# Rows of expert tiles turned by VectorE in 32x32 blocks instead of by TensorE, loaded in five pieces instead of one

## The chip, the cores and the metric

The kernel runs on one core of a Trainium2 chip. The metric is the device time of one execution in microseconds; the profile is of one execution, and its span is the time between its first and last instruction. TensorE (PE), VectorE (DVE), ScalarE (ACT), GpSimd (POOL) and SyncE (SP) each work through a queue of their own in order. SP computes nothing here: it reads registers from tables and issues most of the DMAs.

## The reference

A long convolution, done by Fourier transforms, is followed by a mixture of experts in which each token goes to the one expert with the highest score.

```python
batch, seq, d_model = (8, 5696, 128)          # x; h is (seq, d_model)
N, D, E, F = (45568, 128, 8, 1024)            # w_gate (D, E), w1 (E, D, F), w2 (E, F, D)
...
Xf = np.fft.rfft(x, n=L, axis=1)
Hf = np.fft.rfft(h, n=L, axis=0)
y = np.fft.irfft(Xf * Hf[None, :, :], n=L, axis=1)[:, :S, :]
...
logits = x @ w_gate
expert_idx = np.argmax(logits, axis=1)
...
h = np.maximum(xe @ w1[e], 0.0)
ye = h @ w2[e]
out[mask] = gate_w[mask, None] * ye
```

## The kernel before, in words

The batch is cut in three groups of 2, 3 and 3 sequences. Each goes through a forward transform (`phase_a`), a product with the filter's spectrum (`phase_b`) and the way back with the scoring of tokens (`phase_c`). At the end of `phase_c` GpSimd scatters each token as a row of 130 words into `SR` in DRAM, sorted by expert: 128 values, the gate and the token's index. So each group gives a part of the sorted rows.

`experts()` works on tiles of T = 256 rows, all of one expert, 37 tiles in the first part; 182 tiles lie in the main loop. It runs beside the phases of the later groups: a small scheduler written in Python (`run`) interleaves the generators by costs, and fixes the order of each engine's queue at build time. Once the last group's rows are sorted, expert tiles run alone to the end.

A tile j goes as follows. `load` reads its row number from a table that the chip has computed (`tab`), into a register of SP, and issues the load of 256 rows into a buffer `xr`, two rows to a partition, some three tiles ahead (`ahead(j + 3)`). There are XR = 19 such buffers, used in turn; a few tiles use other free room (`spares`). `turn` makes TensorE flip the two 128x128 halves against an identity matrix (`flip`) into a PSUM bank `mx`, whose other half takes the flips of a finished output `ot`; `turned_in` splits the result into a rounded part (ScalarE) and a rest (VectorE), together `xtb`. Four steps k = 0 to 3 follow: `layer1` fills a PSUM bank `mh` (two of these), `relu` reads it on ScalarE and then on VectorE into `hs`, and two steps later `layer2` adds into `ma`. `drain` copies the sums to `ot`, `turn` flips them back, and `emit` multiplies them by the gate and writes them over the rows in `xr`. `place` later scatters them to `out` by the index that came with the row, two scatters of 128 rows a tile.

Rows of tile j + 1 are turned in step k = 2 of tile j, in the same `turn` as the output of tile j - 1:

```python
jo = j3 if k3 == NPAIR - 1 else None
ji = j + 1 if k == LAG and j + 1 in rows else None
```

The weights of a tile's expert come in four loads `wb` from `WD` (`load_w`), each on the condition that the expert has changed. Up to tile TWO = 76 a tile's weights are asked for one tile ahead, from there two tiles ahead into a second set of buffers. For them SP reads two more numbers of the table. A load waits for the readers of its buffer, and SP's whole queue with it. The DMAs that SP issues signal in turn on eight semaphores, so that each also waits for the one eight before it.

Of the kernel before, what the change touches and what calls it, by code (L numbers as in the profile page):

```python
# [28 lines left out]
T = 256  # L29
# [29 lines left out]
RARE = 3  # L59
TWO = 76  # L60
STEP = 1065
XR = 19
PACE = (1800, 2200)
ROOM = 28
REST = (224, 288, 288)
QUICK = (1, 1, 1)
TABLED = 4
RATE = (0.372, 0.55, 0.28, 0.8, 1.05, 0.6)


@with_exitstack
def conv_moe(ctx: ExitStack, tc: tile.TileContext, I, out, B, S, D, E, F, split):
    nc = tc.nc
# [627 lines left out]

    outs, pending, held = [], [], []

    def place(xr, s, after=None):
        sc = nc.gpsimd.indirect_dma_start(  # L705
            out=out[:, :],
            out_offset=IndirectOffsetOnAxis(ap=xr[:, s, D + 1 : D + 2].bitcast(I32), axis=0),
            in_=xr[:, s, :D],
            in_offset=None,
            bounds_check=B * S - 1,  # L710
            oob_is_err=False,
        ).ins
        tc.declare_no_dep(sc, group="out", reason="each token is written once")
        tc.add_to_no_dep_group("out", sc)
        if len(outs) >= PIPE_LANES:
            tc.add_manual_dep(sc, outs[-PIPE_LANES].name, SYNC, reason="scatter lane")
        if after is not None:
            tc.add_manual_dep(sc, after.name, SYNC, reason="results leave one by one")
        outs.append(sc)

    def spread(done, behind=0):
        gap, now = PACE[0 if state["tail"] else 1], state["pe"] + behind
        if now - state["sent"] < gap:
            return
        if len(pending) > (ROOM if state["space"] else 0):
            place(*pending.pop(0), done.ins)
        elif held and not state["space"]:
            place(*held.pop(0), done.ins)
        else:
            return  # L730
        state["sent"] = now
# [247 lines left out]
    def tables(pt):  # L979
# [62 lines left out]
        tab = const.tile([1, 3, NT], I32, name=f"tab{g}")  # L1042
# [28 lines left out]
        pt.tab = tab  # L1071
# [42 lines left out]
    def experts():  # L1114
# [2 lines left out]
        later, cycle = set(), []  # L1117
        seq = [(pt, j) for pt in parts for j in range(pt.nt)]

        def load(i):  # L1120
            pt, j = seq[i]
            r0 = nc.sync.value_load(pt.tab[0:1, 0, j : j + 1], min_val=0, max_val=E * CAP)
            xr = next(state["spare"], None) if state["spare"] else None
            if xr is None:
                while len(cycle) >= XR and any(o[0] is cycle[-XR] for o in pending):
                    place(*pending.pop(0))
                xr = sb.tile([P, 2, RW], F32, tag="xr", name=f"xr{i}", bufs=XR)
                cycle.append(xr)
            else:
                later.add(i)  # L1130
            ld = nc.sync.dma_start(xr, SR[ds(r0, T), :].rearrange("(p s) w -> p s w", s=2)).ins
            tc.declare_no_dep(ld, group="sr", reason="reads rows that are complete", keep=pt.ends)
            tc.add_to_no_dep_group("rows", ld)
            for s in pt.ends:
                tc.add_manual_dep(ld, s.name, SYNC, reason="all rows are sorted")
            rows[i] = xr

        def turns(i):
# [6 lines left out]
            return wbuf[turns(i), n]  # L1145

        def load_w(i, n):
            pt, j = seq[i]
            if n == 0:
                ew = nc.sync.value_load(pt.tab[0:1, 1, j : j + 1], min_val=0, max_val=(E - 1) * P)  # L1150
                ch = None
                if i and i != TWO + 1:
                    ch = nc.sync.value_load(pt.tab[0:1, 2, j : j + 1], min_val=0, max_val=1)
                regs[i] = (ew, ch)
            ew, ch = regs[i]
# [8 lines left out]
            if n == 3:  # L1164
                regs.pop(i)

        xbank, hbank, obank = {}, {}, {}

        def turn(jo, ji):
            bank = ps.tile([P, 2, 2, P], F32, tag="mx", name=f"mx{jo}_{ji}", bufs=1)  # L1170
            if jo is not None:
                ot = ots.pop(jo)
                for s in range(2):
                    flip(bank[:, 0, s], ot[:, s * P : (s + 1) * P], P)
                obank[jo] = bank[:, 0]
            if ji is not None:
                for s in range(2):
# [48 lines left out]

        def emit(j):
            op, xr = obank.pop(j), rows.pop(j)
            nc.vector.tensor_tensor(
                out=xr[:, :, :D], in0=op, in1=xr[:, :, D : D + 1].broadcast_to([P, 2, D]), op=ALU.mult  # L1230
            )
            if j in later:
                held.extend((xr, s) for s in range(2))
            else:
                pending.extend((xr, s) for s in range(2))

        def tiles(lo, hi):
            LAG = 2
            steps = [(j, k) for j in range(lo, hi) for k in range(NPAIR)]
            hss, wants, due = {}, [], [lo]  # L1240

            def pump():
                while wants and seq[wants[0][0]][0].ready:
                    load_w(*wants.pop(0))

            def want(i, n):
                if i < hi:
                    wants.append((i, n))
                    pt, j = seq[i]
                    if i == TWO or (i == lo and i > TWO and i + 1 < hi):  # L1250
                        wants.append((i + 1, n))
                    pump()

            def ahead(i):
                while due[0] <= min(i, hi - 1) and seq[due[0]][0].ready:
                    load(due[0])
                    due[0] += 1

            while not seq[lo][0].ready:
                yield None  # L1260
            for n in range(4):
                want(lo, n)
            ahead(lo + 2)
            if lo == 0:
                yield LULL
            M = len(steps)
            for n in range(M + LAG + 1):
                j, k = steps[n] if n < M else (None, None)
                j2, k2 = steps[n - LAG] if 0 <= n - LAG < M else (None, None)
                j3, k3 = steps[n - LAG - 1] if n >= LAG + 1 else (None, None)  # L1270
                if k is not None:
                    while not seq[j][0].ready:
                        yield None
                    pump()
                    ahead(j + 3)
                    if j not in xts:
                        turn(None, j)
# [201 lines left out]
```

## Time and profile before

| | us |
|---|---|
| median of 3 runs | 2128.43 |
| lowest and highest | 2121.01, 2129.2 |
| profiled execution | 2119.45 |
| its span | 2117.4 |
| TensorE busy | 2046.9 (97%) |
| VectorE busy | 1563.5 (74%) |
| GpSimd busy | 1347.3 (64%) |
| ScalarE busy | 1119.5 (53%) |

Busy times of TensorE are those of its matmul rows, which overlap; the time that one holds the engine is read from the starts of rows that follow each other. SP's register work and issues are not in the table, since the profile doesn't count them as busy.

### The profile page before, as it was taken

Reading aid. Unit: us, or ns where it says so; the run is one execution under the profiler, and the core shown is the slowest. Engines: PE = TensorE matmul, PEld = TensorE weight load, DVE = VectorE, ACT = ScalarE, POOL = GpSimd, SP = SyncE. Lnnn points to the kernel's source line nnn. Section 1 sums busy time; section 2 is a strip of 40 time slices with the busy share of each in tenths; the row PEclk is TensorE's granted clock in tenths of the full one; section 3 lists DMA queues with packets and bytes.
Section 4 is the critical chain, followed back from the end, with each engine's and each line's share of the span. In section 5 each row is a group of like instructions: output and inputs, shape, how many; then the busy total and the mean of one; then the engine's idle time right before and its main releaser. Section 6 shows DMA issues by size and latency. Waiting matters only on the chain.

```text
span 2117.4 us, 47410 instructions
## 1 busy us (share of the span) xinstructions
PE 2046.9 (97%) x14548; PEld 1779.0 (84%) x14548; DVE 1563.5 (74%) x3520; ACT 1119.5 (53%) x2333; POOL 1347.3 (64%) x1575
## 2 busy tenths in 40 slices
PE   9999999799999999979999999999999999999998
PEld 6799777477777777767888888888889999999998
DVE  5699677799997788889888887677785555555554
ACT  5677555255554544435666665444444444454544
POOL 6576288755554388888998886288884444444333
PEclk9999999799999999999999999999999999999999
DMA  8899799999996898867768775757634144443331
GB/s 268 260 294 304 227 310 284 245 238 228 244 240 194 229 292 254 255 180 209 181 182 221 208 188 149 196 142 205 176 103 143 54 134 136 132 133 130 122 124 34
DMA packets 215138, 415.63 MB, mean 196 GB/s; under 512 B 31797, under 2 KB 135531, under 8 KB 214884
## 3 DMA queue, kind: packets, MB, share of 16 engines
q1 hardware_dynamic: 186703, 357.00, 59.3%
q0 software_dynamic: 27072, 55.35, 9.0%
q8 instruction: 118, 1.93, 0.4%
q14 instruction: 136, 1.11, 0.2%
q10 hardware_dynamic: 1109, 0.23, 0.1%
HBM read 571.44 MB, written 154.27 MB: 343 GB/s over the span
## 4 chain that ended last, share of the span: by engine, by line
PE 78%; DVE 9%; DMA 6%; POOL 3%; issue 2%; ACT 2%; SPq 0%; POOLq 0%; DVEq 0%; ACTq 0%
PE mh L166 22%; PE ma L166 21%; PE vp L166 8%; PE xp L166 8%; PE yp L166 5%; PE pa L166 4%; PE mx L191 3%; POOL SR L687 2%; DMA SR<-rt,pi 1%; DMA uq<-U 1%; DVE hs L1202 1%; DMA wb<-WD 1%; PE lb L191 1%; PE tp L191 1%; PE gb L166 1%
## 5 line engine op out<-in xcount | busy, mean ns | idle before, releaser
L1202 DVE SCALAR_TENSOR_TENSOR hs<-mh,hs 128x512 fp32r<-128x512 f32 x728 | 500.4, 689 | 352.2 <-ACT hs L1200 345.7
L166 PE MATMUL mh<-xtb,wb 128*128 128x256 f32 x4368 | 703.2, 296 | 16.4 <-DVE hs L1202 9.0
L1200 ACT ACTIVATE hs<-mh 128x512 fp32r<-128x512 f32 x728 | 435.6, 599 | 466.7 <-PE mh L166 463.1
L166 PEld LDWEIGHTS mh<-xtb,wb 128*128 128x128 f32 x4368 | 585.9, 189 | 86.2 <-issue 29.9
L166 PE MATMUL ma<-hs,wb 128*128 128x256 f32 x4368 | 653.1, 285 | 3.5 <-DMA wb<-WD 3.5
L166 PEld LDWEIGHTS ma<-hs,wb 128*128 128x128 f32 x4368 | 569.3, 189 | 4.8 <-DMA wb<-WD 4.5
L705 POOL DMA_INDIRECT out<-xr x310 | 305.4, 985 | 347.7 <-ACT hs L1200 164.0
L687 POOL DMA_INDIRECT SR<-rt,pi x384 | 397.8, 1036 | 186.7 <-ACT hs L1200 80.6
L586 POOL TENSOR_TENSOR zt<-zt,xs 128x384 f32<-128x384 f32 (+1 forms) x282 | 300.9, 1069 | 132.2 <-DVE xs L575 93.4
L579 DVE TENSOR_TENSOR xs<-xp,hh 64x384 f32<-64x384 f32 (+1 forms) x360 | 214.7, 596 | 7.8
L623 ACT COPY vt<-vp 96x384 f32<-96x384 f32 x240 | 114.0, 475 | 180.9 <-PE vp L166 177.1
L166 PE MATMUL vp<-zt,mi 128*96 128x384 f32 x480 | 196.2, 490 | 0.7 <-PE xp L166 0.7
L570 DVE TENSOR_TENSOR zt<-xp,hh 128x384 f32<-128x384 f32 (+1 forms) x300 | 173.2, 577 | 25.0 <-PE xp L166 14.7
L166 PE MATMUL xp<-uq,mt 96*128 96x384 f32 (+1 forms) x496 | 173.5, 453 | 16.5 <-DMA uq<-U 10.3
L166 PE MATMUL pa<-xc,fcr 120*120 120x512 f32 x576 | 159.1, 410 | 2.2 <-POOL xc L298 1.0
L166 PE MATMUL yp<-vq,gcs 120*120 120x384 f32 x384 | 140.3, 487 | 4.1 <-ACT ut L331 2.7
L575 DVE SCALAR_TENSOR_TENSOR xs<-xp,hh 64x384 f32<-64x384 f32 x240 | 134.2, 559 | 4.2
L920 POOL MEMSET spent<- 120x288 f32 (+1 forms) x366 | 127.4, 348 | 0.5
L166 PEld LDWEIGHTS pa<-xc,fcr 120*120 120x120 f32 x576 | 98.8, 185 | 25.8 <-DVE rk L909 3.9
L166 PEld LDWEIGHTS xp<-uq,mt 96*128 96x128 f32 x496 | 86.1, 196 | 38.9 <-issue 21.6
L166 PEld LDWEIGHTS vp<-zt,mi 128*96 128x96 f32 x480 | 78.5, 164 | 48.0 <-issue 25.2
L331 DVE COPY ut<-pa 120x512 f32<-120x512 f32 x96 | 65.6, 683 | 64.1 <-PE pa L166 52.8
(168 smaller groups left out, 2587.7 us busy)
## 6 DMA issues: line engine op xcount, KB each, us to landing
wb<-WD SPq DMA_DIRECT2D x728, 512.0 KB
U<-ut SPq DMA_DIRECT2D x48, 720.0 KB
uq<-U SPq DMA_DIRECT2D x60, 576.0 KB
V<-vt SPq DMA_DIRECT2D x60, 576.0 KB
vq<-V SPq DMA_DIRECT2D x48, 720.0 KB
xt<-x SPq DMA_DIRECT2D x96, 240.0 KB
xr<-SR SPq DMA_DIRECT2D x155, 130.0 KB
WD<-wsp SPq DMA_DIRECT2D x32, 512.0 KB
```

The source lines that it names most:

```text
L166: nc.tensor.matmul(to, lhs, rhs, **kw)
L191: nc.tensor.transpose(dst, src, ident[:n, :n])
L570: nc.vector.tensor_tensor(out=zt, in0=x3, in1=hv[:, 0].broadcast_to([P, PK, cb, D]), op=ALU.mult)
L575: nc.vector.scalar_tensor_tensor(out=xs[to, 0], in0=x3[at, 0], scalar=-1.0, in1=him[:, 0], op0=ALU.mult, op1=ALU.mult)
L579: nc.vector.tensor_tensor(out=xs[to], in0=x3[at], in1=him, op=ALU.mult)
L586: eng.tensor_tensor(out=zt, in0=zt, in1=xs, op=ALU.add)
L623: done = nc.scalar.copy(outs_[qb][:, k0 : k0 + PK, c * cw : (c + 1) * cw], banks.pop(n)[:K2, :iw].rearrange("p (q x) -> p q x", q=PK),)
L687: s = nc.gpsimd.indirect_dma_start(out=SR[:, :], out_offset=IndirectOffsetOnAxis(ap=pi[:, b : b + 1], axis=0), in_=rt[:, b, :], in_offset= ...
L705: sc = nc.gpsimd.indirect_dma_start(out=out[:, :], out_offset=IndirectOffsetOnAxis(ap=xr[:, s, D + 1 : D + 2].bitcast(I32), axis=0), in_=x ...
L920: nc.gpsimd.memset(spent[:, : REST[g]], 0.0)
L1200: done = nc.scalar.activation(hs[:, 0], hp, AF.Relu)
L1202: done = nc.vector.scalar_tensor_tensor(out=hs[:, 1], in0=hp, scalar=0.0, in1=hs[:, 0].bitcast(F32), op0=ALU.max, op1=ALU.subtract)
```

## The change

From tile QUAD = 37 on, which is the first tile of the second part, the rows are loaded in five DMAs. Four bring 32 channels each, with the 256 rows as eight blocks of 32 to partitions of their own; the fifth brings gate and index, 8 bytes a row. One VectorE instruction then turns all 32x32 blocks, and since the blocks already lie where the full transpose needs them, the result `xf` is the turned tile. It lies in SBUF, not in PSUM, and no input flip is left on TensorE. The turning moves from step 2 to step 1 of the tile before, and stands on VectorE ahead of that step's `relu`. A partition's two rows are now 128 apart instead of neighbours, so `emit` and `place` see the buffer through `views`. For all tiles, the table is laid out with the three numbers of a tile side by side and read into SP's registers by one instruction (`numbers`). One row buffer gives its room to `xf`.

```diff
-XR = 19
+XR = 18
...
+QUAD = 37
...
+    def views(xr, quad):
+        if not quad:
+            return xr[:, :, :D], xr[:, :, D : D + 1], xr[:, :, D + 1 :]
+        flat = xr.rearrange("p s w -> p (s w)")
+        rest = flat[:, 2 * D :].rearrange("p (s w) -> p s w", w=2)
+        return flat[:, : 2 * D].rearrange("p (s d) -> p s d", d=D), rest[:, :, :1], rest[:, :, 1:]
...
+        def numbers(i):
+            if i not in regs:
+                pt, j = seq[i]
...
+                got = nc.values_load_multi_w_load_instructions(
+                    pt.tab[0:1, j], [mybir.EngineType.SP], min_val=0, max_val=E * CAP, skip_runtime_bounds_check_because=why
+                )[1]
...
         def load(i):
             pt, j = seq[i]
-            r0 = nc.sync.value_load(pt.tab[0:1, 0, j : j + 1], min_val=0, max_val=E * CAP)
+            r0 = numbers(i)[0]
...
+            if i >= QUAD:
+                flat = xr.rearrange("p s w -> p (s w)")
+                for k in range(4):
+                    src = SR[ds(r0, T), k * 32 : (k + 1) * 32].rearrange("(b p) f -> p b f", p=32)
+                    dst = flat[k * 32 : (k + 1) * 32, : 2 * D].rearrange("p (b f) -> p b f", f=32)
+                    moves.append(nc.sync.dma_start(dst, src).ins)
+                src = SR[ds(r0, T), D:].rearrange("(s p) w -> p s w", p=P)
+                moves.append(nc.sync.dma_start(flat[:, 2 * D :].rearrange("p (s w) -> p s w", w=2), src).ins)
...
-            if n == 0:
-                ew = nc.sync.value_load(pt.tab[0:1, 1, j : j + 1], min_val=0, max_val=(E - 1) * P)
...
-                    ch = nc.sync.value_load(pt.tab[0:1, 2, j : j + 1], min_val=0, max_val=1)
...
+        def blocks(j):
+            xbank[j] = sb.tile([P, T], F32, tag="xf", name=f"xf{j}", bufs=1)
+            nc.vector.transpose(xbank[j], rows[j].rearrange("p s w -> p (s w)")[:, : 2 * D])
...
-                ji = j + 1 if k == LAG and j + 1 in rows else None
+                ji = j + 1 if k is not None and k == (1 if j + 1 >= QUAD else LAG) and j + 1 in rows else None
...
-                if jo is not None or ji is not None:
-                    turn(jo, ji)
+                early = ji is not None and ji >= QUAD
+                if jo is not None or ji is not None and not early:
+                    turn(jo, None if early else ji)
...
                 yield 1420
+                if early:
+                    blocks(ji)
                 if k is not None:
                     hss[n] = relu(j, k)
```

VectorE's queue late in the program, where expert tiles run alone, one tile before the change (`hs_0` to `hs_3` are the four steps' buffers, `mx` the PSUM bank of the flips):

```order
L1202 SCALAR_TENSOR_TENSOR hs_1_26283<-mh_1_26270,hs_1_26283 128x512
L1202 SCALAR_TENSOR_TENSOR hs_2_26330<-mh_2_26311,hs_2_26330 128x512
L1185 TENSOR_TENSOR xtb_26336<-mx_109_26318,xtb_26336 128x256
L1229 TENSOR_TENSOR xr_25780<-mx_109_26318,xr_25780 128x2x128
L1202 SCALAR_TENSOR_TENSOR hs_3_26353<-mh_3_26340,hs_3_26353 128x512
L1202 SCALAR_TENSOR_TENSOR hs_0_26385<-mh_0_26372,hs_0_26385 128x512
```

The same place after the change, in VectorE's queue (line numbers have shifted by 30):

```order
L1232 SCALAR_TENSOR_TENSOR hs_0_25383<-mh_0_25370,hs_0_25383 128x512
L1209 STREAM_TRANSPOSE xf_25399<-xr_25160 128x256
L1232 SCALAR_TENSOR_TENSOR hs_1_25401<-mh_1_25386,hs_1_25401 128x512
L1215 TENSOR_TENSOR xtb_25407<-xf_25399,xtb_25407 128x256
L1232 SCALAR_TENSOR_TENSOR hs_2_25431<-mh_2_25414,hs_2_25431 128x512
L1260 TENSOR_TENSOR xr_24959<-mx_None,xr_24959 128x256
L1232 SCALAR_TENSOR_TENSOR hs_3_25451<-mh_3_25438,hs_3_25451 128x512
```

The transpose stands between the `hs` of steps 0 and 1, and the subtraction that makes `xtb` has moved from behind step 2's `hs` to behind step 1's.

SP's queue in the same place before the change, from one tile's first table read to its weight loads (an ISA row is work on registers; semaphore instructions and moves are not listed):

```order
L1122 TENSOR_LOAD tab_25033
L1122 ISA x2
L1131 ISA
L1131 DMA xr_28966<-SR 128x260
L1150 TENSOR_LOAD tab_25033
L1150 ISA x2
L1153 TENSOR_LOAD tab_25033
L1153 ISA x2
L1163 ISA
L1163 DMA wb_0_20374<-WD 128x1024
```

And after the change, SP's queue from the one table read to the first weight load's register work:

```order
L1133 TENSOR_LOAD tab_23308
L1159 ISA
L1159 DMA xr_27887<-SR 32x8x32
L1159 ISA
L1159 DMA xr_27887<-SR 32x8x32
L1159 ISA
L1159 DMA xr_27887<-SR 32x8x32
L1159 ISA
L1159 DMA xr_27887<-SR 32x8x32
L1161 ISA
L1161 DMA xr_27887<-SR 128x2x2
L1191 ISA
```

Two table reads with their register work are gone, and four DMAs with theirs have come.

## Rows read from the trace of the kernel before

**Rows 1.** The page's chain of work that ended last, by engine.
```profile
PE 78%; DVE 9%; DMA 6%; POOL 3%; issue 2%; ACT 2%; SPq 0%; POOLq 0%; DVEq 0%; ACTq 0%
```

**Rows 2.** Windows: busy us (and instructions) by engine, granted clock, DMA share, GB/s.
```profile
986.00:1306.00 320.00, 319.49 (x2156) 280.79 (x2155) 271.26 (x501) 206.10 (x421) 270.84 (x281) 1.00 0.73 195
1306.00:1571.00 265.00, 260.50 (x2184) 225.64 (x2183) 186.90 (x606) 119.07 (x280) 185.91 (x267) 1.00 0.61 165
1571.00:2107.00 536.00, 533.89 (x4517) 532.72 (x4516) 306.53 (x565) 263.39 (x523) 231.45 (x244) 1.00 0.36 115
```

**Rows 3.** Windows of `xtb` alone: PE, PEld, DVE, ACT, then clock and DMA.
```profile
986.00:1571.00 585.00, 240.57 (x1396) 188.91 (x1397) 24.01 (x58) 21.37 (x58) 1.00 0.68 181
1571.00:2107.00 536.00, 305.00 (x2086) 271.69 (x2084) 36.03 (x87) 31.92 (x87) 1.00 0.36 115
```

**Rows 4.** Timeline of TensorE, one late tile: start, duration, line, work.
```profile
1800.18 0.38 PE L191 MATMUL mx<-ident,ot 128*128 128x128 f32 x2
...
1806.29 0.38 PE L191 MATMUL mx<-ident,ot 128*128 128x128 f32 x2
1806.51 0.38 PE L191 MATMUL mx<-ident,xr 128*128 128x128 f32 x2
```

**Rows 5.** Timeline of VectorE in the same tile; in brackets the idle time before.
```profile
1807.12 0.69 DVE L1202 SCALAR_TENSOR_TENSOR hs<-mh,hs 128x512 fp32r<-128x512 f32 x1 [0.72 <-ACT hs L1200]
1807.73 0.42 DVE L1185 TENSOR_TENSOR xtb<-mx,xtb 128x256 fp32r<-128x256 f32 x1
```

**Rows 6.** SP: timeline, then lines L1131, L1150, L1163 (min/median/max ns).
```profile
1803.94 0.34 SPq L1131 DMA_DIRECT2D xr<-SR  x1
1805.81 3.32 SPq L1163 DMA_DIRECT2D wb<-WD  x4
...
L1131 SPq FUSED_REGOPS  x182: 42/42/48, 402.9 to 2085.7; - x182
L1131 SPq MOVE xr<-SR x155: 29/29/42, 410.6 to 2085.9; - x155
L1131 SPq DMA_DIRECT2D xr<-SR x155: 332/343/428, 410.7 to 2086.0; - x155
...
L1150 SPq TENSOR_LOAD <-tab x182: 263/270/1352, 397.5 to 2091.2; - x182
L1150 SPq FUSED_REGOPS  x182: 147/153/187, 398.1 to 2091.5; - x182
L1150 SPq SEQ_ASSERT  x182: 18/18/31, 398.3 to 2091.7; - x182
...
L1163 SPq FUSED_REGOPS  x728: 42/151/171, 398.4 to 2097.4; - x182
L1163 SPq DMA_DIRECT2D wb<-WD x728: 73/81/1852, 398.5 to 2100.1; - x182
L1163 SPq EVENT_SEMAPHORE  x695: 17/17/28, 422.0 to 2097.6; - x174
```

**Rows 7.** SP's issues of two loads with several runs a partition (ns).
```profile
L487 SPq DMA_DIRECT2D uq<-U x90: 317/417/1689, 80.8 to 1279.7; - x90
L752 SPq DMA_DIRECT2D vq<-V x48: 848/930/2432, 684.7 to 1534.2; - x48
```

**Rows 8.** DMA queues (packets, MB, share): first 40 us; whole span.
```profile
q10 hardware_dynamic: 1109, 0.23, 3.2%
...
q1 hardware_dynamic: 186703, 357.00, 59.3%
```

**Rows 9.** Issues counted up to 949 us; timelines of SP and GpSimd near 945 us.
```profile
xr<-SR SPq DMA_DIRECT2D x37, 130.0 KB
out<-xr POOLq DMA_INDIRECT x38
...
942.60 0.36 SPq L1131 DMA_DIRECT2D xr<-SR  x1
...
948.54 1.01 POOL L705 DMA_INDIRECT out<-xr  x1 [0.30 <-DMA SR<-rt,pi]
```

More of the change, by code (lines that the diff above doesn't have):

```diff
@@ L702, in conv_moe, with place @@
     outs, pending, held = [], [], []
-    def place(xr, s, after=None):
+    def views(xr, quad):
[4 more added lines that the diff above has]
+        return flat[:, : 2 * D].rearrange("p (s d) -> p s d", d=D), rest[:, :, :1], rest[:, :, 1:]
+    def place(xr, s, quad, after=None):
+        rows, _, index = views(xr, quad)
         sc = nc.gpsimd.indirect_dma_start(
             out=out[:, :],
-            out_offset=IndirectOffsetOnAxis(ap=xr[:, s, D + 1 : D + 2].bitcast(I32), axis=0),
-            in_=xr[:, s, :D],
+            out_offset=IndirectOffsetOnAxis(ap=index[:, s].bitcast(I32), axis=0),
+            in_=rows[:, s],
             in_offset=None,
@@ L725, in spread @@
         if len(pending) > (ROOM if state["space"] else 0):
-            place(*pending.pop(0), done.ins)
+            place(*pending.pop(0), after=done.ins)
         elif held and not state["space"]:
-            place(*held.pop(0), done.ins)
+            place(*held.pop(0), after=done.ins)
         else:
@@ L1041, in tables @@
         nc.vector.tensor_scalar(out=r0, in0=r0, scalar1=start[:, none : none + 1], scalar2=None, op0=ALU.add)
-        tab = const.tile([1, 3, NT], I32, name=f"tab{g}")
+        pt.tab = const.tile([1, NT, 3], I32, name=f"tab{g}")
+        tab = pt.tab.rearrange("o j k -> o k j")
         nc.vector.tensor_scalar(out=tab[:, 0, :], in0=r0, scalar1=float(E * CAP), scalar2=None, op0=ALU.min)
@@ L1070, in tables @@
         nc.vector.tensor_copy(pt.need, end[:, E - none : E - none + 1])
-        pt.tab = tab
         if not last:
@@ L1118, in experts @@
         seq = [(pt, j) for pt in parts for j in range(pt.nt)]
+        def numbers(i):
+            if i not in regs:
+                pt, j = seq[i]
+                why = "the tables are clamped on the chip"
+                got = nc.values_load_multi_w_load_instructions(
+                    pt.tab[0:1, j], [mybir.EngineType.SP], min_val=0, max_val=E * CAP, skip_runtime_bounds_check_because=why
+                )[1]
+                most = (E * CAP, (E - 1) * P, 1)
+                regs[i] = [
+                    nc.s_assert_within(v, 0, m, skip_runtime_bounds_check_because=why) for v, m in zip(got, most)
+                ]
+            return regs[i]
         def load(i):
             pt, j = seq[i]
-            r0 = nc.sync.value_load(pt.tab[0:1, 0, j : j + 1], min_val=0, max_val=E * CAP)
+            r0 = numbers(i)[0]
             xr = next(state["spare"], None) if state["spare"] else None
@@ L1130, in load @@
                 later.add(i)
[L1131 to L1135, printed above, removed]
+            moves = []
+            if i >= QUAD:
[6 more added lines that the diff above has]
+                moves.append(nc.sync.dma_start(flat[:, 2 * D :].rearrange("p (s w) -> p s w", w=2), src).ins)
+            else:
+                moves.append(nc.sync.dma_start(xr, SR[ds(r0, T), :].rearrange("(p s) w -> p s w", s=2)).ins)
+            for ld in moves:
+                tc.declare_no_dep(ld, group="sr", reason="reads rows that are complete", keep=pt.ends)
+                tc.add_to_no_dep_group("rows", ld)
+                for s in pt.ends:
+                    tc.add_manual_dep(ld, s.name, SYNC, reason="all rows are sorted")
             rows[i] = xr
@@ L1147, in load_w @@
         def load_w(i, n):
-            pt, j = seq[i]
-            if n == 0:
-                ew = nc.sync.value_load(pt.tab[0:1, 1, j : j + 1], min_val=0, max_val=(E - 1) * P)
+            _, ew, ch = numbers(i)
+            if i == 0 or i == TWO + 1:
                 ch = None
-                if i and i != TWO + 1:
-                    ch = nc.sync.value_load(pt.tab[0:1, 2, j : j + 1], min_val=0, max_val=1)
-                regs[i] = (ew, ch)
-            ew, ch = regs[i]
             z = turns(i)
@@ L1163, in load_w @@
             nc.sync.dma_start(dst, WD[n, ds(ew, P), :], **kw)
-            if n == 3:
-                regs.pop(i)
         xbank, hbank, obank = {}, {}, {}
@@ L1228, in emit @@
             op, xr = obank.pop(j), rows.pop(j)
[L1229 to L1235, printed above, removed]
+            to, gate, _ = views(xr, j >= QUAD)
+            nc.vector.tensor_tensor(out=to, in0=op, in1=gate.broadcast_to([P, 2, D]), op=ALU.mult)
+            (held if j in later else pending).extend((xr, s, j >= QUAD) for s in range(2))
         def tiles(lo, hi):
@@ L1276, in tiles @@
                     if j not in xts:
-                        turn(None, j)
+                        blocks(j) if j >= QUAD else turn(None, j)
                         turned_in(j)
                 jo = j3 if k3 == NPAIR - 1 else None
-                ji = j + 1 if k == LAG and j + 1 in rows else None
+                ji = j + 1 if k is not None and k == (1 if j + 1 >= QUAD else LAG) and j + 1 in rows else None
                 if k is not None:
                     layer1(j, k)
-                if jo is not None or ji is not None:
-                    turn(jo, ji)
+                early = ji is not None and ji >= QUAD
+                if jo is not None or ji is not None and not early:
+                    turn(jo, None if early else ji)
                 if k2 is not None:
```

## Prediction

> **What bounds the kernel now.** I read the page's chain first, then cut the part of the span that the change can touch into stretches, then looked at one tile. The chain is TensorE for 78% of the span [rows 1]. The change touches tiles 37 to 181, from about 986 us on. There TensorE is busy 319.49 of 320, 260.50 of 265 and 533.89 of 536 us [rows 2]; the last stretch has weight loads nearly as busy (532.72). Counting ScalarE's casts of turned rows, one a tile, there are 58 tiles up to 1571 us and 87 after it [rows 3]: 145, as many as the change touches.
>
> In the last stretch nothing but expert tiles runs. The flips of two neighbouring tiles start at 1800.18 and 1806.29 us, 6.11 us apart, and nothing in TensorE's rows of that stretch shows idle time [rows 4]. The first flip of an output starts at 1806.29 and the first of an input at 1806.51: two flips hold TensorE for 0.22 us, not for the 0.38 us that a pair's row shows, since they are pipelined [rows 4]. VectorE in the same tile waits 0.72 us for ScalarE before an `hs` of 0.69 us [rows 5]: it has room, and TensorE doesn't wait for it.
>
> **What is taken away.** Two input flips a tile, 0.22 us. In the last stretch TensorE is the bound, so 87 x 0.22 = 19.1 us should come back whole. In the 58 tiles before it TensorE is nearly as full, which is 58 x 0.22 = 12.8 us at most. Together 31.9 us is the ceiling.
>
> **What is added on VectorE.** One transpose of 128x256 f32 a tile, ahead of `hs` at step 1. The trace has none. The nearest row is the 128x256 subtraction, 0.42 us [rows 5]; nothing reads 256 columns for free, so it isn't under some tenths, and if it made two passes over its columns it would be nearer the 0.69 us of the 512-column `hs`. I take 0.42. Its rows are loaded tiles ahead, so it starts when the `hs` before it ends and lies in the idle 0.72 us; both ends fit, and its cost in the last stretch is nothing. If rows came late, it would hold the `hs` behind it in VectorE's queue, then a PSUM bank, then TensorE. In the first stretch VectorE works 271.26 us for 32 tiles [rows 2], 8.5 us a tile of 10.0; with 0.42 to 0.69 more it is 8.9 to 9.2 of 9.8, 91 to 94%. There I don't expect the whole gain.
>
> The Trainium skill ("VectorE: DVE Perf Modes", The three transpose paths) gives 390 ns for TensorE and 311 ns for VectorE on a 128x128 bf16 block, VectorE within 32x32 blocks only. No run here shows VectorE's figure yet; for TensorE the trace differs, with 0.11 us a flip in a row of flips. Two such blocks would be an estimate of 0.62 us, which also fits the 0.72.
>
> **What is added on SP's queue.** One load becomes five, three table reads become one. The price of each, from the medians [rows 6]: between the start of the row load at 1803.94 and of the first weight load at 1805.81 lie 1.87 us, in which stand a load (0.343), two table groups (0.270 + 0.153 + 0.018 each), and 0.151 + 0.017 + 0.029 of the weight load's preparation, 1.42 us in ten instructions. The rest is 0.045 us between instructions. So a table group costs 0.58, the row load with its register work and two semaphore instructions 0.68, a weight load 0.46 (0.081 for the load itself). Before: 3 x 0.58 + 0.68 + 4 x 0.46 = 4.2 us of SP's time in 6.11.
>
> After: one table read without register work behind it (0.27 + 0.045), the first piece 0.68, four more pieces at 0.042 + 0.029 + 0.343 + 3 x 0.045 = 0.55, and the weights: 0.32 + 0.68 + 2.20 + 1.83 = 5.0 us in a tile of 6.11 - 0.22 = 5.89. The issue of a piece has no row. Its shape, 32 partitions of eight short runs, is nearest to `uq` (96 of four runs, 0.417 us); with that it is 5.4 us. If the register work before each piece costs the 0.151 of a weight load in place of 0.042, it is 5.8. The upper end is `vq`, 0.930 us [rows 7], and 8.0 us. I take 5.4: SP keeps up, with half a microsecond left where it had two. The limit is at 0.515 us a piece. Behind SP's pieces wait the weight loads of the next tiles; in the last stretch these are two tiles ahead, so a microsecond late costs nothing. Before tile 76 they are one tile ahead, and at a change of expert the lateness may show: I put 1 us for all of it.
>
> **What is added on the DMA engines.** 1280 packets, of 128 and 8 bytes, in place of 128 of 1040. The nearest row of short packets is the constants' queue: 1109 packets of 0.23 MB take 3.2% of 16 engines in 40 us [rows 8], 18.5 ns each. 1280 of them over 16 engines are 1.5 us a tile. The other end is the average of the main queue, 186703 packets in 59.3% of 2117.4 us [rows 8], 108 ns, 8.6 us a tile; its packets are some ten times longer, so I take 18.5 ns. The last stretch has a DMA share of 0.36 [rows 2], 2.2 us a tile; 3.7 of 5.9 still hides. In the first it is 0.73 of 10.0 us, and 8.8 of 9.8 after. There, with VectorE and SP fuller too, I write off a third of the 12.8 us.
>
> The rule that speaks against the pieces is in the Trainium skill ("DMA: Bandwidth & Descriptors", Specifications): a transfer under 512 B doesn't reach line rate. If by it a piece is billed as 512 B at about 27 GiB/s an engine, 1280 pieces are an estimate of 1.4 us a tile, which would leave the sum as it is; no run here shows the billing.
>
> **What one buffer less does.** With 18 row buffers the load of tile 36 reuses tile 18's, and waits until both its scatters have left. Up to 949 us there are 37 row loads and 38 scatters [rows 9]: the last row load is tile 36's, at 942.60, and the last scatter is tile 18's second, at 948.54 for 1.01 us. So SP stands for 949.55 - 942.60 = 7 us, once, with the next group's `uq` loads and the weight loads behind it. TensorE feels between nothing (they are loaded ahead) and all 7 us; half, 3.5. Other loads reach buffers long since free.
>
> The tables' other layout and the later `emit` view move as many elements by as many instructions as before: nothing.
>
> **Sum.** -31.9 + 4.3 (a third of 12.8) + 3.5 + 1 = -23.1 us. The profiled execution took 2119.45 us (span 2117.4); it would become 2096. The median shown is 2128.43, 0.4% above it, and against the median the forecast is 2105. About 0.5% (11 us) is what a measurement can tell here from no change.
>
> **The rivals.**
> - *SP becomes the bound.* It decides from 0.515 us a piece. For it: 5.4 to 5.8 us of 5.89 is thin, and `vq` shows that an SP issue can take 0.93. Against it: the row load itself and `uq` are under the limit. At 0.65 us a tile takes 5.0 + 5 x 0.31 = 6.6 us, and the last stretch alone loses 87 x 0.4 = 36 us: 2160. At 0.93 it loses 87 x 1.8 = 160: 2285.
> - *The DMA engines become the bound.* From (5.9 - 2.2) x 16 / 1280 = 46 ns a packet. At the main queue's 108 ns a tile takes 8.6 + 2.2 = 10.8 us and the stretch loses 87 x 4.7 us: over 2500. Against it is the 18.5 ns, taken while the engines were loaded.
> - *The middle gives nothing.* VectorE or late loads take the 12.8 us of the 58 tiles, and the stand at tile 36 costs its 7: -19.1 + 7 + 1 = -11, 2117.
> - *The flips were not on the path.* If the pace of a tile is set by weight loads or by the chain through `hs`, nothing comes back: 2128. Against it is that a flip also loads weights, and that the flips' 0.22 us stand in the row between matmuls.
>
> **How the numbers follow.** Forecast 0.60; middle gives nothing 0.13, on the edge of 0.5%, half to faster; no gain 0.07; SP 0.15, most of it slower, 0.02 about even; DMA 0.05. Faster 0.60 + 0.07 = 0.67, same 0.06 + 0.07 + 0.02 = 0.15, slower 0.18. The range goes from the ceiling with a little scatter (2128 - 32 - 2 = 2094) to no change (2130), and leaves out the two slower rivals; the forecast alone lies between 2096 and 2113.
>
> **What would show it.** Tiles after 1571 us at 5.9 us apart with one pair of flips; a VectorE transpose under 0.72 us that starts right behind `hs`; SP's pieces under 0.5 us each; a DMA share in the last stretch up from 0.36 to 0.6 or less; a stand of SP near 943 us. Wrong would be: tiles 6.1 us apart or more with TensorE waiting for rows or weights (SP or DMA), or `hs` late behind the transpose.

## The result, and the profile after

The changed kernel takes 2138.03 us (median of 6 runs, 2132.53 to 2143.04) beside 2125.6 us of the kernel before: ratio 1.0056, interval 1.0036 to 1.0077. A second measurement (`f1_after`) gave 2138.77 beside 2127.32, 1.0043 (1.0028 to 1.0057). It is slower by about half a per cent, where 23 us less were forecast.

The chain and the three windows of the changed kernel, which answer to [rows 1, 2] (columns as there):

```profile
PE 67%; DVE 10%; DMA 9%; POOL 6%; issue 3%; ACT 3%; SPq 2%; POOLq 0%; ACTq 0%; DVEq 0%
...
986.00:1306.00 320.00, 309.73 (x2011) 267.42 (x2010) 284.27 (x511) 195.95 (x404) 263.96 (x275) 0.98 0.79 188
1306.00:1571.00 265.00, 251.17 (x2017) 214.43 (x2016) 191.02 (x587) 116.77 (x272) 173.82 (x245) 0.99 0.69 169
1571.00:2107.00 536.00, 525.52 (x4430) 516.65 (x4429) 348.14 (x705) 261.13 (x534) 247.47 (x270) 1.00 0.47 117
```

TensorE's share of the chain fell from 78 to 67%, DMA and GpSimd gained. In the first window TensorE idles 10 us in place of half a microsecond, in the second 14 in place of 4.5. The granted clock, third from the end of a line, is no longer 1.00 there. What TensorE waits for is in its list of waits over the whole span (total us, times, longest):

```profile
PE xp L167 <- DMA uq<-U: 12.9, 5, 7.5
PE mx_None L192 <- ACT ot L1255: 12.3, 13, 1.8
PE mh L167 <- DVE hs L1232: 12.2, 18, 2.6
PE mh L167 <- DMA wb<-WD: 9.5, 5, 3.5
PE ma L167 <- DMA wb<-WD: 4.0, 5, 1.4
```

And the waits for `hs` and for weights in the same list before:

```profile
PE mh L166 <- DVE hs L1202: 9.0, 12, 2.5
PE ma L166 <- DMA wb<-WD: 3.5, 5, 1.4
PE mh L166 <- DMA wb<-WD: 1.4, 1, 1.4
```

One entry is new, the output flips that wait for ScalarE's copy `ot`, and the waits for weights have grown from 4.9 to 13.5 us. The late stretch, by contrast, looks as forecast. Its timelines answer to [rows 4, 5]: TensorE, then VectorE.

```profile
1800.78 0.84 PE L167 MATMUL mh<-xtb,wb 128*128 128x256 f32 x6
1801.48 0.44 PE L192 MATMUL mx_None<-ident,ot 128*128 128x128 f32 x2
1801.67 0.93 PE L167 MATMUL ma<-hs,wb 128*128 128x256 f32 x6
```

```profile
1800.16 0.44 DVE L1209 STREAM_TRANSPOSE xf<-xr 128x256 f32<-128x256 f32 x1
1800.89 0.69 DVE L1232 SCALAR_TENSOR_TENSOR hs<-mh,hs 128x512 fp32r<-128x512 f32 x1 [0.29 <-ACT hs L1230]
1801.49 0.41 DVE L1215 TENSOR_TENSOR xtb<-xf,xtb 128x256 fp32r<-128x256 f32 x1
...
1806.02 0.43 DVE L1209 STREAM_TRANSPOSE xf<-xr 128x256 f32<-128x256 f32 x1
```

One pair of flips is left, the transpose takes 0.43 us in what was idle time, and the next tile's stands 5.86 us later. SP's issues, the first counterpart of [rows 6], are cheaper than priced; only the read of three numbers is dearer (ns, min/median/max):

```profile
L1159 SPq DMA_DIRECT2D xr<-SR x472: 316/326/1682, 960.5 to 2104.7; - x158
...
L1161 SPq DMA_DIRECT2D xr<-SR x118: 389/395/1577, 962.7 to 2105.2; - x118
...
L1133 SPq TENSOR_LOAD <-tab x182: 662/674/2265, 395.7 to 2102.1; - x182
```

Where the time went is read from the start of each tile's `ot` copy in the two traces. Between the copies of tiles 36 and 102 lie 633.4 us before and 659.5 us after, 26 more; from tile 102 to the last, 482.9 before and 467.6 after, 15 less. (In the second profile of the changed kernel it is 655.3 and 472.8.) **The last stretch gained, the middle lost more.**

### The profile page after: what moved, and what is told of

The parts are those of the page before. It is cut to its first block, busy times and chain, and to the rows that moved or that the text cites. A ratio compares the mean times of both kernels' runs of the same rounds, so it can differ in the third digit from the quotient of the medians.

```text
span 2133.4 us, 47975 instructions
## 1 busy us (share of the span) xinstructions
PE 2031.3 (95%) x14258; PEld 1750.2 (82%) x14258; DVE 1630.5 (76%) x3665; ACT 1110.3 (52%) x2333; POOL 1348.1 (63%) x1575
## 4 chain that ended last, share of the span: by engine, by line
PE 67%; DVE 10%; DMA 9%; POOL 6%; issue 3%; ACT 3%; SPq 2%; POOLq 0%; ACTq 0%; DVEq 0%
PE mh L167 19%; PE ma L167 19%; PE vp L167 7%; PE xp L167 7%; PE yp L167 4%; POOL SR L688 3%; PE pa L167 3%; DMA SR<-rt,pi 3%; PE mx_None L192 2%; DMA wb<-WD 2%; DVE hs L1232 1%; DVE xs L580 1%; PE lb L192 1%; DMA uq<-U 1%; POOL spent L929 1%
## 5 line engine op out<-in xcount | busy, mean ns | idle before, releaser
L167 PE MATMUL mh<-xtb,wb 128*128 128x256 f32 x4368 | 702.8, 297 | 28.0 <-DVE hs L1232 12.2
L587 POOL TENSOR_TENSOR zt<-zt,xs 128x384 f32<-128x384 f32 (+1 forms) x282 | 301.0, 1069 | 134.6 <-DVE xs L576 90.8
```

Of the source, the lines that this page charges most:

```text
L167: nc.tensor.matmul(to, lhs, rhs, **kw)
L587: eng.tensor_tensor(out=zt, in0=zt, in1=xs, op=ALU.add)
```

## The experiments

Theories after the result, all for the middle: *late loads* (the five loads a tile), *order* (ScalarE's cast of the turned rows stands ahead of the `ot` copy and waits for VectorE), *port* (VectorE's subtraction is slowed beside GpSimd), *stand* (SP held by the missing buffer). Ratios are to the kernel before, measured in the same job. e1 to e4 stood on one chip, e10 to e13 on a second, f1 to f4 on a third; the others stood on one on which the kernel before takes 2150 us. So only ratios are compared across jobs, and a ratio of 0.001 is 2 us.

| run | what is kept | us | ratio (interval) |
|---|---|---|---|
| e1_flips | table read and 18 buffers only | 2123.31 | 0.9973 (0.9958, 0.9989) |
| e13_xr19 | table read only | 2121.85 | 0.9973 (0.9959, 0.9987) |
| e2_one_load† | transposes, one load | 2115.58 | 0.9941 (0.9919, 0.9962) |
| e3_pieces† | five loads, TensorE's flips | 2145.59 | 1.0071 (1.0046, 1.0095) |
| e11_one_drain† | transposes, one load, `ot` copy first | 2098.8 | 0.9861 (0.9838, 0.9884) |
| e4_psum | whole change, transpose into PSUM | 2189.23 | 1.0287 (1.0257, 1.0317) |
| e9_tail | whole change from tile 104 | 2132.95* | 0.9924 (0.9898, 0.9950) |
| e12_tail_drain | the same, `ot` copy first | 2108.22 | 0.9908 (0.9889, 0.9928) |
| f1_after / f2_drain | whole change / `ot` copy first | 2138.77 / 2132.54 | 1.0043 / 1.0014 (1.0000, 1.0029) |
| f3_five_long / f4_sp_time | flips; five whole-row loads / three more reads | 2144.08 / 2132.6 | 1.0065 (1.0047, 1.0082) / 1.0020 (1.0009, 1.0031) |
| g1_five_32 / g2_sp_time | the same pair, loads of 32 and 16 partitions | 2176.92* / 2151.71* | 1.0114 (1.0078, 1.0150) / 1.0006 (0.9983, 1.0029) |

(* on the chip with 2150 us. † what is turned isn't the layout that the multiplication wants, so other numbers are computed; these are measurements, no kernels to use.)

**Parts of the change alone.** `e1_flips` sets the first tile to be turned beyond the last:

```diff
-QUAD = 37
+QUAD = 999
```

> All tiles keep TensorE's flips and the one row load; only one buffer less, the one table read a tile and the tables' layout are left of the change. Four theories share the 26 us that tiles 36 to 102 lost: port (VectorE's subtraction slowed beside GpSimd), order (ScalarE's cast ahead of the output copy), late loads (the pieces on SP and DMA), stand (SP held at tile 36's load by the missing buffer, and the dearer table read). Stand says slower than before by 5 to 8 us, nearly all of it lost by tile 37: about 2132. The three others say that only the 3.5 us of the prediction or less are here: 2126 to 2129.

Faster than before, not slower: *stand* is no cause of the loss.

`e13_xr19` differs from it by `XR = 19`.

> As the run in which TensorE flips all inputs and one table read is left, but with 19 row buffers again: against it, this is what the missing buffer costs. By the prediction the stand of SP at tile 36's load costs 3.5 us (0 to 7): 0.9973 - 0.0016 = 0.996 (0.994 to 0.997). If the stand is hidden: 0.997.

The same ratio as e1, each with an interval of 0.0015 to either side: the buffer's cost doesn't show, though a cost of the forecast size (0.0016) isn't excluded. What is left of the change in e13 is one table read in place of three, with the tables' layout, and it gains 0.27% (5.7 us).

```diff
-            if i >= QUAD:        # e2: load in one piece, emit to match
+            if i >= 999:
```

> VectorE's transposes stay, but a tile's rows are loaded in one piece, two rows a partition, as before; what is transposed is then not the layout that the multiplication wants, so other numbers are computed, in the same time otherwise. Late loads says that the middle comes back: some 20 us or more under the change, 2118 or less. Port and order say that the middle stays lost: 2133 to 2138, with the subtraction still at up to 2.3 us between 986 and 1320 us. The last stretch gains 0.19 us a tile as with the change under all of them.

```diff
-                        blocks(j) if j >= QUAD else turn(None, j)    # e3: flips at step 2
+                        turn(None, j)
```

> The five-piece loads from tile 37 on stay, but TensorE flips the inputs at step 2 as before (of the pieces' layout, so other numbers are computed); VectorE transposes nothing. Late loads says that the middle's loss is here without a gain: 2126 + 5 for the stand + about 20 = 2150. Port and order say no loss beyond the stand: 2131. A tile of the last stretch should take as long as before in both, with SP and DMA hidden there.

The five loads cost 1.0071 - 0.9973 = 0.0098 with TensorE's flips, and 1.0056 - 0.9941 = 0.0115 or 1.0043 - 0.9941 = 0.0102 with VectorE's transposes: 21 to 24 us either way. *Late loads* holds: between tiles 36 and 102 the profile of e3 takes 656.5 us, that of e1 633.1. But without pieces the transposes gain only 0.9973 - 0.9941 = 0.0032, 7 us. The parts nearly add up: 0.9973 - 0.0032 + 0.0098 = 1.0039.

**ScalarE's order.** In the changed kernel, around 1069 us (all engines' timeline):

```profile
1069.01 0.45 DVE L1209 STREAM_TRANSPOSE xf<-xr 128x256 f32<-128x256 f32 x1
1069.49 0.69 DVE L1232 SCALAR_TENSOR_TENSOR hs<-mh,hs 128x512 fp32r<-128x512 f32 x1
1069.49 0.41 ACT L1214 CAST xtb<-xf 128x256 fp32r<-128x256 f32 x1 [1.93 <-DVE xf L1209]
1069.80 0.36 ACT L1255 COPY ot<-ma 128x256 f32<-128x256 f32 x1
...
1070.22 0.44 PE L192 MATMUL mx_None<-ident,ot 128*128 128x128 f32 x2 [0.70 <-ACT ot L1255]
```

ScalarE stands 1.93 us for a transpose that VectorE reaches late; the `ot` copy behind it is late by as much, and TensorE's output flips wait. Over the run ScalarE waits 43.1 us for the transposes, 44 times. `e5_drain` (f2_drain again) and `e11_one_drain` put the copy first:

```diff
                     hss[n] = relu(j, k)
+                if k2 == NPAIR - 1:
+                    drain(j2)
+                if k is not None:
                     if ji is not None:
                         turned_in(ji)
...
-                if k2 == NPAIR - 1:
-                    drain(j2)
```

> All of the change, but at step 1 ScalarE's copy of the output half of the tile before (ot) stands ahead of its cast of the transposed rows, which waits for VectorE; between 986 and 1590 us TensorE's output flips waited 8.3 us for that copy with the change and none before. Order says that these 8 us come back: 2128 to 2131, and no wait of the output flips for ot is left. Port (the subtraction slowed beside GpSimd, which then makes everything behind VectorE late) says that the wait moves to hs and the time stays: 2136 to 2139.

1.0024 (0.9997 to 1.0052), 2151.9 us on the chip of 2150: within the expectation of *order* as a ratio, but no proof, so it was run again beside the changed kernel:

> The whole change with ScalarE's ot copy ahead of its cast, again, beside the whole change on the same chip. The order change was worth 0.0080 where rows came by one load (0.9941 to 0.9861). If it is worth the same beside the pieces: 0.008 under the changed kernel's ratio, 0.998. If the pieces' late loads hide it: 0.003 under, 1.002 to 1.003.

> One load a tile (the turned data isn't the rows, as in the first run with one load) with VectorE's transposes, and ScalarE's ot copy ahead of its cast of the transposed rows. Without the order change the ratio was 0.9941. If order was all that kept the middle from gaining, its 58 tiles give back 0.22 us each beside the last stretch's: 0.988 to 0.990. If it was the port (the subtraction of up to 2.3 us beside GpSimd, which stays): 0.992 to 0.995, with hs or ma waits in place of those for ot.

With one load the ratio falls by 0.0080, 17 us. But the two runs stood on different chips, and in their profiles 6.8 us of the difference lie ahead of tile 36's `ot` copy, where no row is transposed yet; 7.0 lie between tiles 36 and 102 and 3.5 behind them. So some 10 us are the order's. Beside the pieces, on one chip, it is worth 0.0029, 6 us, and in the profiles none of that lies between tiles 36 and 102 (655.3 and 656.4 us). What takes its place can be seen. TensorE's waits between 986 and 1590 us: of e2_one_load, e11_one_drain, f1_after and f2_drain, and at the end its wait for `hs` before the change.

```profile
PE mx_None L192 <- ACT ot L1255: 8.3, 11, 1.5
PE mh L167 <- DVE hs L1232: 6.3, 14, 0.9
```

```profile
PE mh L167 <- DVE hs L1232: 9.7, 16, 1.6
PE ma L167 <- ACT us L558: 2.2, 1, 2.2
PE ma L167 <- DMA wb<-WD: 1.4, 2, 0.9
```

```profile
PE mx_None L192 <- ACT ot L1255: 8.3, 9, 1.6
...
PE mh L167 <- DMA wb<-WD: 3.9, 3, 1.9
```

```profile
PE mh L167 <- DMA wb<-WD: 12.2, 4, 4.6
PE mh L167 <- DVE hs L1232: 7.4, 14, 1.6
```

```profile
PE mh L166 <- DVE hs L1202: 2.8, 8, 0.4
```

The wait for `ot` is gone in both with the copy first. With one load little takes its place, but TensorE still waits for VectorE, 9.7 us for `hs` in place of 2.8 before the change; with the pieces TensorE runs into the weights, 12.2 in place of 3.9 us.

**What five loads cost.** `e7_five_long` (f3 again) loads whole rows by 26, 26, 26, 25 and 25 partitions, `e8_short` loads 128-byte runs by two loads and the gates by a third, `e10_sp_time` (f4, g2 again) has SP read the table anew ahead of the weight loads 0, 2 and 3:

```diff
+                for lo, hi in ((0, 26), (26, 52), (52, 78), (78, 103), (103, P)):      # e7
+                    moves.append(nc.sync.dma_start(xr[lo:hi], src[lo:hi]).ins)
...
+            _, ew, ch = numbers(i, (1, 1, 2, 3)[n] if i >= 37 else 0)                  # e10
```

> TensorE flips all inputs, as in the run with one load and one buffer less (2123, ratio 0.9973 to before); from tile 37 on a tile's rows come by five loads of 25 or 26 partitions each, in whole rows of 1040 bytes, so SP issues as often as with the change and the DMA engines move as few packets as before. If the loss by pieces is SP's time to issue: as with pieces and TensorE's flips, 1.0071, 2140 to 2146. If it is the short packets: 2123 to 2126.

> TensorE flips all inputs; from tile 37 on a tile's rows come by two loads of 512 runs of 128 bytes, and the gates and indices by a third of 8-byte runs: as many short packets as with the change, by three issues in place of five (a tile's elements stand in another order, so other numbers are computed). If the loss by pieces is the short packets: as with pieces and TensorE's flips, 1.0071, 2140 to 2146. If it is SP's time to issue: half of the way from 2123 to 2146, 2134, or less.

> TensorE flips all inputs and the rows come by one load (0.9973 to before in the first such run); from tile 37 on SP reads the table three times more a tile, ahead of the first, third and fourth weight load, at 0.67 us a read and some register work: about 2.1 us more of SP's time a tile, as much as four more pieces took, with no more transfers. If the pieces cost by SP's time: the same loss as five whole-row loads, 1.007 to 1.009. If they cost by the eight semaphores that SP's transfers take in turn (each issue waits until the transfer eight issues earlier has landed, so that more issues a tile bring that wait nearer): no loss, 0.997 to 1.000.

e7: 1.0086 (1.0058 to 1.0114), e8: 1.0102 (1.0068 to 1.0136), both on the chip of 2150; e10: 1.0033 (1.0017 to 1.0049). Whole rows cost as much as short runs, so short packets aren't needed for the loss. e8 tells SP's time and the count of loads apart only poorly: its three issues take 0.383 us twice and 0.564, five of e7's take 0.311 each, and SP's own instructions between 986 and 1320 us sum up to 182 us in e8, 191 in e7 and 136 with one load. Why e8 isn't a little cheaper than e7 stays open. SP's time without transfers costs only part. On one chip:

> TensorE flips, five loads of whole rows a tile from tile 37 on, again, beside the run that only keeps SP busy, on the same chip. Where SP's time is all: the same ratio as that run, 1.003. Where the eight semaphores' waits come on top: 1.007 to 1.009.

> TensorE flips, one load a tile and three more table reads a tile from tile 37 on, again: SP has at least as much to do as with five loads, but no more transfers. 1.003 as before; the distance to the run with five whole-row loads is what the transfers themselves cost, by their eight semaphores: 0 if SP's time is all, 0.004 to 0.006 if not.

1.0065 against 1.0020: 0.0045, 10 us, for transfers beyond SP's time, and 1.0020 - 0.9973 = 0.0047, 10 us, for the time (by e10 and e13, on one chip, 0.0060). Both theories hold, about half each. A pair with even partition counts guards against uneven loads being the reason:

> As the run with TensorE's flips and five loads of whole rows a tile, but of 32, 32, 32, 16 and 16 partitions in place of 26, 26, 26, 25 and 25. Uneven partition counts might spread a transfer over fewer DMA engines and land it later; if that was part of the five loads' cost, the distance to the run that only keeps SP busy shrinks: 1.002 to 1.004. If the count of transfers alone makes it: 1.006 to 1.009.

1.0114 against 1.0006: the uneven counts are not the reason. On this chip the distance is larger, 0.0108, or 0.0080 from e7's 1.0086.

The mechanism is in the program's order of SP. Every transfer counts on one of eight semaphores, taken in turn, and an issue waits until the transfer eight issues earlier has landed. Five issues in a row of the changed kernel's middle, with what each waits for (DMAHW0 to DMAHW7 are the eight, Pool is GpSimd's semaphore):

```
L1159 DMA xr_14124<-SR 32x8x32 [waits DMAHW3_49]
L1161 DMA xr_14124<-SR 128x2x2 [waits DMAHW4_49]
L488 DMA uq_44_14178<-U_74 96x4x384 [waits DMAHW5_49,Pool_49]
L491 DMA mi_121<-miq 48x384 [waits DMAHW6_49]
L491 DMA mi_121<-miq 48x384 [waits DMAHW7_49]
```

SP's waits for transfers between 986 and 1320 us, first of f3_five_long, then of f4_sp_time:

```profile
SPq L1187 <- DMA uq<-U: 11.4, 8, 2.2
SPq L1157 <- DMA uq<-U: 3.7, 5, 1.6
SPq L1187 <- DMA wb<-WD: 3.6, 3, 1.9
```

```profile
SPq L1191 <- DMA uq<-U: 2.4, 3, 2.0
SPq L666 <- DMA uq<-U: 0.4, 1, 0.4
```

L1187 and L1191 are weight loads, L1157 the row pieces. No weight or row load reads `uq`: what they wait for is a semaphore that an attention load still holds. Summed over SP's idle gaps of more than 0.08 us in front of an instruction that waits for these semaphores alone, from 986 to 1590 us: 9.3 us before, 12.0 in e1, 41.7 after, 45.7 in f3, 4.0 in f4. SP's own instructions, those on semaphores left out, between 986 and 1320 us take 136 us in e1, 203 after, 191 in f3 and 222 in f4: f4 keeps SP busier than the pieces do and yet loses less.

What this costs TensorE is more than the waits. Windows from tile 36's `ot` copy to tile 102's, in which TensorE has the same matmuls to do in all runs that keep its flips: before, e1_flips, e3_pieces, f3_five_long, f4_sp_time, and then the changed kernel (columns as in [rows 2]).

```profile
994.58:1627.96 633.38, 626.26 (x4733) 552.73 (x4732) 488.27 (x1187) 345.47 (x741) 478.49 (x576) 1.00 0.66 178
1004.09:1637.17 633.08, 626.85 (x4733) 553.16 (x4732) 488.33 (x1187) 345.37 (x740) 479.39 (x576) 1.00 0.67 178
1005.44:1661.89 656.45, 633.98 (x4733) 558.45 (x4732) 489.21 (x1187) 345.30 (x740) 479.23 (x576) 0.99 0.71 172
1006.24:1666.15 659.91, 637.64 (x4733) 561.68 (x4732) 489.87 (x1187) 345.59 (x740) 480.34 (x576) 0.98 0.66 172
995.66:1640.14 644.48, 629.83 (x4733) 555.01 (x4732) 489.22 (x1187) 345.78 (x740) 480.66 (x576) 1.00 0.67 175
999.40:1658.91 659.51, 625.79 (x4595) 544.57 (x4594) 526.63 (x1252) 342.39 (x741) 477.16 (x573) 0.98 0.71 171
```

Five loads make this part 23.4 us longer (e3 against e1): TensorE idles 16.2 us more, and the same 4733 matmuls keep it busy 7.1 us longer. The second part goes with the granted clock. In the changed kernel it stands at 0.50, the lower of its two levels (1.2 in place of 2.4 GHz), in five stretches of this window, 20.5 us in all. TensorE has waited 1.7 to 3.5 us ahead of each, three times for weights. In e3 it is 13.7 us, in f3 23.9, in f4 3.4, and before and in e1, e2 and e11 none. One such stretch in the changed kernel, as a window and in TensorE's rows:

```profile
1227.00:1233.70 6.70, 6.24 (x23) 5.54 (x24) 2.34 (x6) 1.85 (x5) 2.96 (x3) 0.50 0.96 250
...
1224.90 0.95 PE L167 MATMUL mh<-xtb,wb 128*128 128x256 f32 x6 [1.76 <-DMA wb<-WD]
1227.46 1.65 PE L167 MATMUL ma<-hs,wb 128*128 128x256 f32 x6 [1.38 <-DMA wb<-WD]
...
1230.57 2.06 PE L167 MATMUL mh<-xtb,wb 128*128 128x256 f32 x6
...
1234.72 1.17 PE L167 MATMUL mh<-xtb,wb 128*128 128x256 f32 x6
```

Six matmuls into `mh` take 2.06 us in it, 0.95 before it and 1.17 behind it. Of the 15.4 us by which f3's window is longer than f4's, 7.6 are idle time and 7.8 longer matmuls.

**The port.** The subtraction `xtb` now reads `xf` from SBUF. VectorE and GpSimd around 1059 us in the changed kernel, and the subtraction's sum over 986 to 1320 us:

```profile
1059.46 1.04 POOL L560 TENSOR_TENSOR us<-uq,us 96x384 fp32r<-96x384 f32 x1
1059.62 2.14 DVE L1215 TENSOR_TENSOR xtb<-xf,xtb 128x256 fp32r<-128x256 f32 x1
1060.44 1.03 POOL L587 TENSOR_TENSOR zt<-zt,xs 128x384 f32<-128x384 f32 x1
...
986.00:1320.00 334.00, 24.23 (x32) 0.98 0.78 187
```

24.23 us for 32, 0.76 each, in place of 0.41. The one that takes 2.14 starts 0.16 us after `us` and ends 0.29 us after `zt`: it lies beside nearly all of the two. `e4_psum` lets the transpose write into the free half of the output flips' bank:

```diff
-            xbank[j] = sb.tile([P, T], F32, tag="xf", name=f"xf{j}", bufs=1)
+            bank = ps.tile([P, 2, 2, P], F32, tag="mx", name=f"mxf{j}", bufs=1)
+            half.append(bank)
+            xbank[j] = bank[:, 1].rearrange("p s t -> p (s t)")
```

> The transpose writes into the free half of the output flips' PSUM bank in place of SBUF, so that VectorE's subtraction reads one operand from PSUM, as before the change. Port says that the subtraction falls back to 0.42 us throughout and the middle gives back the 11 us of its excess and what waited behind it: 2110 to 2127. Order and late loads say about as with the change, 2135 to 2138, with the subtraction at 0.42 all the same. If the transpose itself, which then writes to PSUM, is dearer than 0.43 us, a few us go the other way.

```profile
L1217 DVE TENSOR_TENSOR xtb<-mxf,xtb 128x256 fp32r<-128x256 f32 x32 | 13.2, 414 | 0.0
...
PE mxf L192 <- DVE xtb L1217: 26.7, 61, 0.4
```

With PSUM as the source the subtraction is back at 0.414 us each. As a test of the time it failed: the shared bank makes the output flips wait for the subtraction, 26.7 us between 1700 and 2100 us alone (second line), and the kernel is 61 us slower than before. So no run shows the port's price. In e11, which ends at 0.9861, the subtraction still takes 27.50 us for 34, and TensorE waits 9.7 us for `hs` in place of 2.8: VectorE is late by the longer subtraction or by the transpose ahead of it, which no run separates.

**Where it pays.**

> The change from tile 104 on, where nothing but expert tiles runs; tiles before it are loaded in one piece and flipped by TensorE. If port, order and late loads cost only beside the attention work of the middle, the last stretch's gain is left: 78 tiles at 0.15 to 0.22 us are 12 to 17 us under the 2123 of the run in which every tile is flipped by TensorE: 2106 to 2112, faster than both kernels. If the pieces or the transposes cost in the last stretch too: 2120 or more.

> The change from tile 104 on, and ScalarE's ot copy ahead of its cast. Without the order change the ratio was 0.9924. Order cost the change 8.3 us between 986 and 1590 us, and in the last stretch about 4; if those 4 come back, 0.990 to 0.991; if TensorE is the bound there whatever ScalarE's order, 0.992 to 0.993.

0.9924 and 0.9908: with the transposes only from tile 104 on, where SP has no attention loads to issue, the change takes some 16 and 20 us less than the kernel before, 5.7 of them by the table read. The 4 us between the two, for the order, are within the intervals.

## Why the prediction was wrong, by its steps

- **The flips: right.** In the run with one load and the copy first, a tile of the last stretch takes 5.863 us (68 tiles, from the starts of the `ot` copies), with flips and the same buffers 6.084: 0.221 us, forecast 0.22. In the changed kernel it takes 5.94 us, in e2 5.91.
- **The transpose: price right, cover too simple.** 0.434 us, forecast 0.42. "Its cost in the last stretch is nothing" holds; what was overlooked is ScalarE's queue, where the cast waits for the transpose with the `ot` copy behind it. The step asked who waits for `hs` behind the transpose, not who stands behind the cast. It is worth 10 to 17 us where nothing else is late. The third of 12.8 us written off in the middle was too little even then: 633.1 us from tile 36 to 102 with flips, 629.0 with e11, 4 us of the 14.5 that 66 tiles would give (one profile each). TensorE's waits for `hs` grew there; whether by the lengthened subtraction or by the transpose isn't shown.
- **SP: the step that failed.** The prediction checked SP in the last stretch, where 5.4 of 5.89 us fit, and they do. For the stretch before it said that lateness may show and "I put 1 us for all of it". That term measures 21 to 24 us; in e3's profile 16.2 of 23.4 are TensorE's longer idle time and 7.1 its lower clock, for which the prediction has no term. SP also issues the attention's loads there, which the step didn't count, and each issue waits on the semaphore of the eighth before it, which the count of issues changes and their price doesn't. The eight semaphores were known ahead of the prediction; its sum of SP's time has no wait for them. The rival "SP becomes the bound" named the engine, but its threshold of 0.515 us a piece was not reached by the medians (0.326 and 0.395; its 87 x 0.4 is 35, not 36). The rival "The middle gives nothing" named late loads, but let them take no more than the 12.8 us of the flips. The prediction's sign of being wrong, tiles 6.1 us apart or more, belongs to the last stretch, where the forecast held (5.94).
- **The DMA engines: right.** A 128-byte packet takes 14.5 ns (33792 of them between 986 and 1320 us), forecast 18.5; the last stretch's share is 0.50 in the trace's window of 1700 to 2100 us, forecast 0.6 or less. Five loads of whole rows cost as much (f3 1.0065, e3 1.0071), so the loss doesn't come from short packets.
- **The missing buffer: nothing that shows in sum.** The load of tile 36, at 942.60 us before [rows 9], starts at 947.80, but the weight loads ahead of it are 3.4 us late already (943.82 in place of 940.40), so the stand itself is some 2 us. On e13's chip the traces with 18 buffers reach tile 36's `ot` copy 4 to 5 us later than e13 (998.4 to 999.3 in place of 994.5), but in the last stretch they take 6.08 in place of 6.13 us a tile with flips, and the ratios of e1 and e13 are equal.
- **The tables: not nothing.** One read of 0.67 us in place of three groups of 0.58 [rows 6] saves SP a microsecond a tile, and e1 and e13 gain 5.7 us. That it is SP's time that gains them, as it is lost with the pieces, is argued and not shown.

The sum as measured: -5.7 (table read), -7 (transposes, as ordered), +21 to 24 (five loads) make +8 to 11, beside +9 to 12 for the whole; forecast -23.1. With the copy first and no pieces, e11 stands 24 us under e1 (21 in the profiles from tile 36 on), of 27.6 forecast for the flips: most of that gain is there, and the loads take it back. The parts add up only as ordered: with the copy first the five loads cost more (f2 against e11, on two chips: 1.0014 - 0.9861 = 0.0153, 33 us).

## What to carry to other kernels

Price an issue not only by its own time: count how many transfers stand between an issue and the one whose semaphore it reuses, in the stretch where the queue carries most, and ask what the oldest of them is. When an operation moves to another engine, follow the in-order queue of its consumer too, and see what stands behind the one that now waits. A change that gains in one stage and loses in another can be switched on from a tile number: here that turned +0.5% into -0.8%, of which 0.3% is the table read. And a wait of TensorE may cost more than its length: look at the granted clock behind it.

## What the runs showed of the hardware

- VectorE's 128x256 subtraction with both operands in SBUF takes up to 2.34 us beside GpSimd's additions, 0.414 with one operand in PSUM. This fits the shared, exclusive port of the Trainium skill ("SBUF — State Buffer", Who interferes with whom), which names an operation with two SBUF inputs against a GpSimd operation that reads SBUF; the trace agrees.
- A register load of three numbers takes 0.674 us, of one 0.270 [rows 6].
- With 18 row buffers in place of 19, and TensorE busy the whole time in both, a tile of the last stretch takes 6.084 in place of 6.132 us. The matmuls into `mh` average 280 and 281 ns there. The cause stays open.
- Behind waits of TensorE of 1.7 to 3.5 us its granted clock fell to 0.50 (1.2 GHz) for 3.4 to 6.8 us, five times between tiles 36 and 102 of the changed kernel; six matmuls of 256 columns took 2.06 us there and 0.95 at 1.00.
- On a chip where the kernel before takes 1% longer (2150 us), the transfers' part of the loads' cost is 0.0080 to 0.0108 (0.004 to either side) in place of 0.0045 (0.002). Why that chip is slower wasn't sought.
